# A written instruction order for the first sequence of a thresholded-attention and ELU-FFN kernel

## The chip, the cores and the metric

The kernel runs on one core of one Trainium2 chip. A core has five engines, each with a queue of its own: PE (TensorE, matrix products and transposes, into PSUM), DVE (VectorE), ACT (ScalarE), POOL (GpSimd) and SP (SyncE, which here issues the DMAs). They meet through semaphores. The metric is the device time of one execution in microseconds; lower is better.

## The reference

Two blocks follow each other. The attention block has 8 batch elements ("sequences") of 8 heads, 576 rows, head size 64. Of each row of scores only those within tau of the row's maximum are kept:

```
scores = scale * np.matmul(q, k.transpose(0, 1, 3, 2))
thresh = np.max(scores, axis=-1, keepdims=True) - tau
scores = np.where(scores >= thresh, scores, -1000000000.0)
attn = np.exp(scores - np.max(scores, axis=-1, keepdims=True))
attn = attn / (np.sum(attn, axis=-1, keepdims=True) + 1e-09)
return np.matmul(attn, v).astype(np.float32)
```

The result, 4608 tokens by 512, goes through `h = x @ w_in` (512 by 2048), an ELU, and `@ w_out` (2048 by 512). The two weight matrices arrive as 64-bit floats and are turned into 32-bit ones on the core.

## The kernel before

**Steps.** Two heads make a pair; a sequence has 4 pairs, all sequences 32. The 576 rows of a pair are worked in five steps, i = 0 to 4. Steps 0 to 3 take 128 rows of both heads; step 4 takes the last 64 rows of both heads as one tile of 128 rows (`heads_of(4)` is `[0]`). A sequence is thus 20 steps and 36 tiles of a head; `per_seq` is 20.

**One head of a step.** `scores` (L238, PE) writes 128 by 576 scores to PSUM. The row maximum `mx` (L248, DVE) gives `nb`, the negative scaled maximum (L249, POOL), and the threshold `th` (L250, POOL). The exponential `e` is on ACT (L253), with `nb` as its bias. The mask (L265, DVE) keeps `e` where the score reaches `th`, writes `w` and sums it into `sm`. DVE adds 1e-9 and takes the reciprocal `rs` (L267, L268), and POOL multiplies `w` by it (L274).

**From w to the output.** `turn_parts` turns `w` in three parts: PE transposes (L277) into a PSUM tile `rt`, and ACT copies it to `wTa` (steps 0 and 1) or `wTb` (steps 2 to 4) (L293). `values` multiplies the turned tiles with v (L384, L388) into a PSUM tile `pv`, once a pair for steps 0 and 1 (part 0) and once for steps 2 to 4 (part 1). ACT copies that to `xt`, for part 1 to `xs` as well (L395, L400). `behind(pr, i)` does this for a step that completes a part and nothing for the others.

**Loads.** `load` brings q, k and v of a pair by DMAs on SP: four for q (`qm`), four for k (`km`), four for v. DVE transposes q and k (`prep_q` L195, `prep_k` L200), and POOL makes small copies (`copy_q` L207, `copy_k` L212).

**Weights.** Each matrix is cut into 16 pieces. `load_w` brings one; its conversion has the parts `convert_rest` (ACT, L129), `convert_top` (DVE, L136 and L137), `convert_add` (POOL, L143), `convert_abs` (ACT, L148) and `convert_end` (DVE, L155). `progress` counts the pieces loaded and converted. In the first sequence, calls of `convert_w` take six pieces, one each at head tiles 12, 16, 20, 24, 28 and 32.

**Buffers.** In the first sequence PSUM holds three tiles of scores for one head each (pool `ps_s0`, six of eight banks) and two tiles shared by `rt` and `pv` (pool `ps_t`).

**Three stages and their order.** The first sequence (20 steps) runs by head tiles in a loop that calls `begin` (scores and exponential) of tile n+1 before `finish` (mask and normalization) of tile n. This loop isn't in a manual schedule: a scheduler puts its instructions in order on each engine. The second stage (15 steps, with the rest of the weights and the first FFN products) and the third are inside `tc.manual_schedule()`: there each engine has its instructions in the order of the code. The functions `max_of`, `bound_of`, `exp_of`, `mask_of` and `reciprocal_of` are defined for the third stage (L1076 to L1104); there `nb` is made by ACT (L1086).

Of the kernel before, what the change touches and what calls it, by code (L numbers as in the profile page):

```python
# [10 lines left out]
FP32 = mybir.dt.float32  # L11
# [3 lines left out]
ALU = mybir.AluOpType  # L15
# [4 lines left out]
def kernel(  # L20
# [55 lines left out]


    tau_sb = const.tile([P, 1], FP32, name="tau_sb")
    nc.sync.dma_start(tau_sb, tau.to_broadcast([P, 1]))
    pos = const.tile([P, 1], FP32, name="pos")  # L80
    nc.vector.tensor_scalar(pos, tau_sb, 0.0, None, ALU.is_ge)
    keep = const.tile([P, 1], FP32, name="keep")
    nc.vector.tensor_scalar(keep, pos, SCALE, None, ALU.mult)
    nkeep = const.tile([P, 1], FP32, name="nkeep")
    nc.vector.tensor_scalar(nkeep, pos, -SCALE, None, ALU.mult)
    far = const.tile([P, 1], FP32, name="far")
    nc.vector.tensor_scalar(far, pos, -FAR, FAR, ALU.mult, ALU.add)
    ntau = const.tile([P, 1], FP32, name="ntau")
    nc.vector.tensor_tensor(ntau, tau_sb, far, ALU.max)
    nc.vector.tensor_scalar(ntau, ntau, -1.0 / SCALE, None, ALU.mult)  # L90

    w_in_sb = const.tile([P, KJ, DF], FP32, name="w_in_sb")
    w_out_sb = const.tile([P, NFT, DM], FP32, name="w_out_sb")
# [17 lines left out]
    def load_w(ahead=2):  # L111
        i = progress[0]
        if i >= len(pieces) or i >= progress[1] + ahead:
            return
        progress[0] += 1
        src, dst, j, n = pieces[i]
        rows = src[j * P : (j + 1) * P]
        if src.dtype == FP32:
            nc.sync.dma_start(dst, rows[:, n : n + WN])
            return  # L120
        st = staged[i] = wstage.tile([P, WN, 2], U32, name="wst", bufs=4)
        nc.sync.dma_start(st.rearrange("p n w -> p (n w)"), rows.bitcast(U32)[:, 2 * n : 2 * (n + WN)])
# [6 lines left out]
            nc.scalar.mul(lo.bitcast(I32), lo, 2.0**-29)  # L129

    def convert_top(i):

        if i in staged:
            hi = staged[i][:, :, 1]
            top = tops[i] = wstage.tile([P, WN], U32, name="wtop", bufs=2)
            nc.vector.tensor_scalar(top, hi, 3, 0x3FFFFFFF, ALU.logical_shift_left, ALU.bitwise_and)  # L136
            nc.vector.scalar_tensor_tensor(top, hi, 0xC0000000, top, ALU.bitwise_and, ALU.bitwise_or)  # L137

    def convert_add(i):
# [14 lines left out]
            mag, top = staged.pop(i)[:, :, 1].bitcast(FP32), tops.pop(i).bitcast(FP32)  # L154
            nc.vector.scalar_tensor_tensor(pieces[i][1], mag, 1.125 * 2.0**-15, top, ALU.is_ge, ALU.mult)  # L155

    def convert_w():
        i = progress[1]
        if i >= progress[0]:
            return  # L160
        for f in (convert_top, convert_rest, convert_add, convert_abs, convert_end):
            f(i)
        load_w()


    raws, pairs = {}, {}


    def load(pr, parts=("qm", "km", "v"), shared=False):
        b, j = divmod(pr, NPAIR)  # L170
        tiles = raws.setdefault(pr, {})
        for name, src in (("qm", q), ("km", k)):
            if name not in parts:
                continue
            m = tiles[name] = raw.tile([P, S // T, T], FP32, name="qm" if shared else name)
            for i in range(2):
                for d in range(2):
                    r = (2 * i + d) * T
                    nc.sync.dma_start(
                        m[r : r + T],  # L180
                        src[b, 2 * j + i].rearrange("(j t) d -> t j d", t=T)[:, :, d * T : (d + 1) * T],
                    )
        if "v" not in parts:
            return
        vm = tiles["vm"] = raw.tile([P, 2, NC, D], FP32, name="vm", bufs=2)
        vd = tiles["vd"] = vds[pr % NVD]
        for i in range(2):
            vh = v[b, 2 * j + i]
            nc.sync.dma_start(vm[:, i], vh[:MAIN].rearrange("(c p) d -> p c d", p=P))
            r = slice(i * TAIL, (i + 1) * TAIL)  # L190
            nc.sync.dma_start(vd[r, r], vh[MAIN:])
# [22 lines left out]
    def prep(pr):  # L214
        for f in (prep_q, copy_q, prep_k, copy_k):
            f(pr)
# [5 lines left out]
    def scores(pr, i, hs):  # L222
        qT, kT, qd = pairs[pr]
        if hs[0] == 0:
            open_steps[pr, i] = {
                **{x: small.tile([P, 2], FP32, name=x) for x in ("mx", "nb", "th", "sm", "rs")},
            }
        st = open_steps[pr, i]
        if "f" in psum and not apart:
            both = psum["s"].tile([P, 2, 2, 512], FP32, name="sc")  # L230
            scs = {h: both[:, h] for h in hs}
        else:
            scs = {h: psum["s"].tile([P, 2, 512], FP32, name="sc") for h in hs}
        for a in range(2):
            for h in hs:
                k0 = a * HALF + (0 if h else TAIL)
                r, qs = (slice(h * D, (h + 1) * D), qT[:, i * P : (i + 1) * P]) if i < NC else (slice(0, P), qd)
                nc.tensor.matmul(scs[h][:, a, :HALF], qs[r], kT[r, k0 : k0 + HALF], start=True, stop=True)  # L238
        if len(hs) == 2 and not apart:
            st["both"] = both  # L240
        for h in hs:
            st[h] = scs[h]
# [27 lines left out]
    def normalize(pr, i, hs):  # L270
        st = open_steps[pr, i]
        for h in hs:
            wv = st["w"][:, h * S : (h + 1) * S]
            nc.gpsimd.tensor_scalar(wv, wv, st["rs"][:, h : h + 1], 1.0, ALU.mult, ALU.mult)  # L274

    def transpose(dst, src):
        nc.tensor.matmul(dst, src, ident, is_transpose=True, skip_group_check=True)  # L277

# [7 lines left out]


    def turn_parts(pr, i):
        w = open_steps.pop((pr, i))["w"]
        wT, g0 = turned_tile(pr, i)  # L290

        def to(gs, cs, src, r=slice(0, P)):
# [213 lines left out]
    def heads_of(i):  # L506
        return [0, 1] if i < NC else [0]
# [28 lines left out]
            for post in posts[engines]:  # L536
                post()

    def begin(*step):
        scores(*step)  # L540
        exponentials(*step)

    def finish(*step):
        masks(*step)
        normalize(*step)

    def ahead(pr, i):
        if i == 2 and pr + 1 < NP:
            prep(pr + 1)
        if i == 3 and pr + 2 < NP:  # L550
            load(pr + 2, ("qm", "km"))
        if i == 3 and pr + 1 < NP and pr:
            load(pr + 1, ("v",))

    load(0)
    prep(0)
    load(1)

    heads = [(pr, i, [h]) for pr, i in steps[:per_seq] for h in heads_of(i)]
    turned = deque()  # L560
    begin(*heads[0])
    for n, (pr, i, hs) in enumerate(heads):
        if n + 1 < len(heads):
            begin(*heads[n + 1])
        if n == 2:
            load_w()
            load_w()
        if n >= 12 and n % 4 == 0:
            convert_w()
        finish(pr, i, hs)  # L570
        if len(turned) > 1:
            behind(*turned.popleft())
        if n and hs == [0]:
            turn(*heads[n - 1][:2])
            turned.append(heads[n - 1][:2])
        if hs == [1]:
            ahead(pr, i + 1)
    first.close()
    for name, bufs in (("s", 1), ("f", 2)):
        psum[name] = banks.enter_context(tc.tile_pool(name=f"ps_{name}", bufs=bufs, space=PSUM))  # L580

    while len(turned) > 1:
        behind(*turned.popleft())

# [159 lines left out]
    with tc.manual_schedule():  # L746
# [326 lines left out]
                    at(end + lag, f)  # L1073
                n -= 1

        def max_of(pr, i, h):  # L1076
            st = open_steps[pr, i]
            nc.vector.tensor_reduce(st["mx"][:, h : h + 1], st[h][:, :, :HALF], axis=AX.XY, op=ALU.max)  # L1078

        def bound_of(pr, i, h):  # L1080
            st = open_steps[pr, i]
            nc.gpsimd.tensor_scalar(st["th"][:, h : h + 1], st["mx"][:, h : h + 1], 1.0, ntau, ALU.mult, ALU.add)  # L1082

        def exp_of(pr, i, h):
            st = open_steps[pr, i]
            nc.scalar.mul(st["nb"][:, h : h + 1], st["mx"][:, h : h + 1], nkeep)  # L1086
            e = att.tile([P, 2, HALF], FP32, name="e")
            nc.scalar.activation(e, st[h][:, :, :HALF], AF.Exp, bias=st["nb"][:, h : h + 1], scale=keep)  # L1088
            st[h] = st[h], e

        def mask_of(pr, i, h):
            st = open_steps[pr, i]
            if h == 0:
                st["w"] = wpool[0].tile([P, 2 * S], FP32, name="w")
            sc, e = st.pop(h)
            wv = st["w"][:, h * S : (h + 1) * S].rearrange("p (a n) -> p a n", a=2)
            nc.vector.scalar_tensor_tensor(wv, sc[:, :, :HALF], st["th"][:, h : h + 1], e, ALU.is_ge, ALU.mult,  # L1097
                                           accum_out=st["sm"][:, h : h + 1])

        def reciprocal_of(pr, i, hs):  # L1100
            st = open_steps[pr, i]
            cs = slice(hs[0], hs[-1] + 1)
            nc.vector.tensor_scalar(st["sm"][:, cs], st["sm"][:, cs], 1e-9, None, ALU.add)
            nc.vector.reciprocal(st["rs"][:, cs], st["sm"][:, cs])  # L1104

        begun = [0.0]

        def softmax(pr, i):
# [143 lines left out]
```

## Time and profile before

| what | us |
|---|---|
| median of 3 runs (lowest, highest) | 1387.35 (1385.84, 1392.01) |
| the profiled execution's own time | 1385.93 |
| its span in the profile | 1384.1 |

| engine | busy in the span, us | share |
|---|---|---|
| PE, matmuls | 1334.5 | 96% |
| DVE | 1066.5 | 77% |
| POOL | 827.5 | 60% |
| ACT | 632.4 | 46% |

All other numbers come from this profiled execution. Times are counted from the start of its span. A line of the timeline has a start, a duration, the engine, the line of the code, the operation, what it writes from what it reads with shapes, how many instructions were merged, and, in brackets, how long the engine stood idle before it and what released it. A line of the windows view has, for one stretch, the busy time and the number of instructions of PE, PE's weight loads, DVE, ACT and POOL, then the granted clock of PE, the share of the DMA engines and GB/s. Ends of matmuls are modelled, so a busy PE is not a PE at its peak. Float32 matmuls are recorded in two instructions each; transposes in one.

### The profile page before, as it was taken

How to read it: one execution, taken by the hardware profiler on the slowest of the kernel's cores; microseconds unless marked ns; L12 is line 12 of the kernel's file. 1: busy time of each engine (PE TensorE's matmuls, PEld its weight loads, DVE VectorE, ACT ScalarE, POOL GpSimd, SP SyncE). 2: the span in 40 equal slices, each digit the busy share in tenths (PEclk: the TensorE clock that was granted, in tenths of full speed). 3: DMA queues.
4: the chain of work that ended last, by engine and by line, in shares of the span. 5: the costliest groups of instructions: out<-in, count | busy, mean ns of one | idle time of the engine just before them, and what ended most of it. 6: DMA issues, size and time to landing. Idle time of an engine off the chain costs nothing.

```text
span 1384.1 us, 21954 instructions
## 1 busy us (share of the span) xinstructions
PE 1334.5 (96%) x6566; PEld 988.6 (71%) x6566; DVE 1066.5 (77%) x2362; ACT 632.4 (46%) x1387; POOL 827.5 (60%) x1331
## 2 busy tenths in 40 slices
PE   6897989999999999999999999999999999999998
PEld 4554745747777777777777777777777777888886
DVE  6877885988888887888788978888888874545533
ACT  4666654325454445445453636263635452422421
POOL 5667773878657564756475747675666656414422
PEclk9999999999999999999999999999999999999999
DMA  5245451688897979898888988897889785411211
GB/s 114 58 91 148 132 148 44 187 244 254 226 261 221 280 214 255 209 266 240 230 231 256 251 222 236 236 258 212 239 230 275 217 241 146 133 58 64 92 57 31
DMA packets 316342, 259.82 MB, mean 188 GB/s; under 512 B 208320, under 2 KB 272320, under 8 KB 316224
## 3 DMA queue, kind: packets, MB, share of 16 engines
q1 hardware_dynamic: 316224, 258.42, 67.4%
q8 instruction: 53, 0.87, 0.3%
q14 instruction: 65, 0.53, 0.1%
HBM read 167.84 MB, written 90.51 MB: 187 GB/s over the span
## 4 chain that ended last, share of the span: by engine, by line
PE 76%; DVE 9%; ACT 5%; POOL 4%; issue 3%; DMA 1%; SPq 1%; DVEq 0%; POOLq 0%; ACTq 0%
PE f L999 28%; PE f L846 21%; PE sc L238 11%; PE pv L388 9%; PE pv L384 2%; PE f L435 2%; PE f L475 2%; ACT e L1088 2%; DVE w L265 2%; ACT e L253 1%; DVE mx L1078 1%; PE rt L277 1%; POOL wtop L143 1%; DVE mx L248 1%; DVE wtop L137 1%
## 5 line engine op out<-in xcount | busy, mean ns | idle before, releaser
L274 POOL TENSOR_SCALAR w<-w,rs 128x576 f32<-128x576 f32 x288 | 246.2, 860 | 108.4 <-DVE rs L1104 75.1
L1078 DVE TENSOR_REDUCE mx<-sc 128x1 f32<-128x576 f32 x207 | 148.0, 751 | 82.6 <-PE sc L238 82.6
L238 PE MATMUL sc<-kT,qT 64*128 64x288 f32 x1024 | 182.6, 440 | 22.1 <-DVE w L265 11.9
L348 DVE STREAM_TRANSPOSE x<-w 128x512 f32<-128x512 f32 (+1 forms) x350 | 182.5, 567 | 8.2 <-POOL w L274 8.2
L1086 ACT ACTIVATE nb<-mx,nkeep 128x1 f32<-128x1 f32 x207 | 61.4, 297 | 253.4 <-DVE mx L1078 253.4
L1088 ACT ACTIVATE e<-sc,nb,keep 128x576 f32<-128x576 f32 x207 | 172.1, 831 | 6.9
L1097 DVE SCALAR_TENSOR_TENSOR w<-sc,th,e 128x576 f32<-128x576 f32 x207 | 163.0, 810 | 8.6 <-ACT e L1088 0.4
L238 PEld LDWEIGHTS sc<-kT,qT 64*128 64x128 f32 x1024 | 100.7, 191 | 87.2 <-issue 51.8
L846 PE MATMUL f<-xt,sw 128*128 128x256 f32 x512 | 129.0, 389 | 1.0 <-DVE ot L1017 0.5
L846 PE MATMUL f<-xt,w_in_sb 128*128 128x256 f32 x512 | 125.1, 383 | 1.7 <-ACT w L860 1.5
L1082 POOL TENSOR_SCALAR th<-mx,ntau 128x1 f32<-128x1 f32 x207 | 54.3, 263 | 111.6 <-DVE mx L1078 111.4
L846 PEld LDWEIGHTS f<-xt,sw 128*128 128x128 f32 x512 | 93.2, 190 | 29.8 <-issue 13.5
L846 PE MATMUL f<-x,w_in_sb 128*128 128x256 f32 x448 | 109.0, 382 | 5.5 <-ACT g L913 5.5
L253 ACT ACTIVATE e<-sc,nb,keep 128x576 f32<-128x576 f32 x81 | 65.1, 830 | 104.2 <-POOL nb L249 103.2
L846 PEld LDWEIGHTS f<-xt,w_in_sb 128*128 128x128 f32 x512 | 95.7, 190 | 22.1 <-ACT xs L400 4.6
L999 PE MATMUL f<-w_out_sb,s 128*128 128x256 f32 x448 | 109.4, 387 | 0.0
L999 PE MATMUL f<-t,s 128*128 128x256 f32 x448 | 106.7, 381 | 0.6 <-POOL s L939 0.6
L999 PE MATMUL f<-w_out_sb,g 128*128 128x256 f32 x448 | 107.2, 382 | 0.0
L846 PEld LDWEIGHTS f<-x,w_in_sb 128*128 128x128 f32 x448 | 84.1, 190 | 21.2 <-ACT g L913 10.2
L999 PEld LDWEIGHTS f<-w_out_sb,s 128*128 128x128 f32 x448 | 82.3, 190 | 23.0 <-issue 13.2
L999 PEld LDWEIGHTS f<-w_out_sb,g 128*128 128x128 f32 x448 | 84.0, 190 | 15.8 <-ACT ge L879 3.5
L999 PEld LDWEIGHTS f<-t,s 128*128 128x128 f32 x448 | 84.0, 190 | 14.3 <-POOL s L939 3.4
(162 smaller groups left out, 2543.6 us busy)
## 6 DMA issues: line engine op xcount, KB each, us to landing
there<-x SPq DMA_DIRECT2D x500, 144.0 KB, 4.2
wTb<-there SPq DMA_DIRECT2D x75, 576.0 KB, 4.6
wTa<-there SPq DMA_DIRECT2D x50, 576.0 KB, 4.3
sw<-win_sums SPq DMA_DIRECT2D x62, 384.0 KB, 4.7
t<-wout_sums SPq DMA_DIRECT2D x45, 512.0 KB, 5.4
qm<-in_q_dram SPq DMA_DIRECT2D x128, 72.0 KB, 4.2
vm<-in_v_dram SPq DMA_DIRECT2D x64, 128.0 KB, 4.2
wst<-in_moe_w_in_dram SPq DMA_DIRECT2D x16, 512.0 KB, 4.5
```

What stands on the lines that cost most here:

```text
L238: nc.tensor.matmul(scs[h][:, a, :HALF], qs[r], kT[r, k0 : k0 + HALF], start=True, stop=True)
L253: nc.scalar.activation(e, st[h][:, :, :HALF], AF.Exp, bias=st["nb"][:, h : h + 1], scale=keep)
L274: nc.gpsimd.tensor_scalar(wv, wv, st["rs"][:, h : h + 1], 1.0, ALU.mult, ALU.mult)
L348: nc.vector.transpose(x[:, :, c0 : c0 + nc_], src.rearrange("p (c g n) -> p g c n", c=nc_, n=T))
L388: nc.tensor.matmul(pv[h * D : (h + 1) * D, g0 * T : g1 * T], vm[:, h, c], wT[:, g0:g1, h * (NC + 1) + c], start=False, stop=(c == NC - 1), ...
L846: nc.tensor.matmul(loc["banks"][place], left[:, j], right[:, j], start=(begins and j == 0), stop=(j == 1), skip_group_check=True)
L999: nc.tensor.matmul(place(m), lhs, rhs, start=(begins and v == 0), stop=(v == RU - 1), skip_group_check=True)
L1078: nc.vector.tensor_reduce(st["mx"][:, h : h + 1], st[h][:, :, :HALF], axis=AX.XY, op=ALU.max)
L1082: nc.gpsimd.tensor_scalar(st["th"][:, h : h + 1], st["mx"][:, h : h + 1], 1.0, ntau, ALU.mult, ALU.add)
L1086: nc.scalar.mul(st["nb"][:, h : h + 1], st["mx"][:, h : h + 1], nkeep)
L1088: nc.scalar.activation(e, st[h][:, :, :HALF], AF.Exp, bias=st["nb"][:, h : h + 1], scale=keep)
L1097: nc.vector.scalar_tensor_tensor(wv, sc[:, :, :HALF], st["th"][:, h : h + 1], e, ALU.is_ge, ALU.mult, accum_out=st["sm"][:, h : h + 1])
```

## The change

It rewrites the first stage; the second and third are left as they are.

- The first stage is put into `tc.manual_schedule()` and goes by steps of two heads instead of by head tiles: one call of `scores` for both heads, then maximum, bound, exponential and mask of each head at written places, and one reciprocal for both.
- ACT makes `nb` of head 0 (`nc.scalar.mul`), POOL that of head 1.
- The turning of step n-1 stands in step n: its first part ahead of head 1, its others behind the scores of step n+1. `behind(n-2)` stands after the reciprocal. The five parts of a weight's conversion are spread over steps; the loads stand at steps i = 3 and 4.
- At the start q is issued first on SP, then tau, and k of the first pair on ACT's queue. The instructions that read tau come after the first transposes of q and k. PE makes 28 transposes of the identity into a tile that nobody reads.
- The functions of the third stage are moved up, and `exp_of` gets a parameter `on_pool`.

```diff
-    nc.sync.dma_start(tau_sb, tau.to_broadcast([P, 1]))
...
-    load(0)
-    prep(0)
-    load(1)
...
-    begin(*heads[0])
-    for n, (pr, i, hs) in enumerate(heads):
-        if n + 1 < len(heads):
-            begin(*heads[n + 1])
-        if n == 2:
-            load_w()
-            load_w()
-        if n >= 12 and n % 4 == 0:
-            convert_w()
-        finish(pr, i, hs)
-        if len(turned) > 1:
-            behind(*turned.popleft())
-        if n and hs == [0]:
-            turn(*heads[n - 1][:2])
-            turned.append(heads[n - 1][:2])
-        if hs == [1]:
-            ahead(pr, i + 1)
+    with tc.manual_schedule():
+        load(0, ("qm",))
+        nc.sync.dma_start(tau_sb, tau.to_broadcast([P, 1]))
+        load(0, ("km",), queue=nc.scalar)
+        load(0, ("v",))
+        load(1)
+
+        idle = psum["t"].tile([P, NC, P], FP32, name="rt", tag="rt")
+        for _ in range(28):
+            transpose(idle[:, 0], ident)
+        prep_q(0)
+        prep_k(0)
+        read_tau()
+        copy_k(0)
+        copy_q(0)
+        scores(0, 0, [0, 1])
+        for n in range(per_seq):
+            pr, i = steps[n]
+            hs = heads_of(i)
+            x = progress[1]
+            if n:
+                normalize(*steps[n - 1], [0])
+                turned = turn_parts(*steps[n - 1])
+            max_of(pr, i, 0)
+            exp_of(pr, i, 0)
+            bound_of(pr, i, 0)
+            if n:
+                copies = turned[0]()
+            if len(hs) == 2:
+                max_of(pr, i, 1)
+                st = open_steps[pr, i]
+                nc.gpsimd.tensor_scalar(st["nb"][:, 1:], st["mx"][:, 1:], nkeep, 1.0, ALU.mult, ALU.mult)
+            if n and len(heads_of(steps[n - 1][1])) == 2:
+                normalize(*steps[n - 1], [1])
+            if len(hs) == 2:
+                exp_of(pr, i, 1, True)
+                bound_of(pr, i, 1)
+            if n:
+                copies()
+
+            if i == NB - 1 and n + 1 < per_seq:
+                convert_top(x)
+                convert_add(x)
+            elif i == 0 and n:
+                convert_end(x)
+                load_w()
+            elif i == 1 and pr:
+                convert_sign(x)
+                convert_add(x)
+            elif i in (2, 3):
+                (prep_q if i == 2 else prep_k)(pr + 1)
+                (copy_q if i == 2 else copy_k)(pr + 1)
+            mask_of(pr, i, 0)
+            if n + 1 < per_seq:
+                scores(*steps[n + 1], heads_of(steps[n + 1][1]))
+            if n:
+                for part in turned[1:]:
+                    part()()
+            if len(hs) == 2:
+                mask_of(pr, i, 1)
+            reciprocal_of(pr, i, hs)
+            if n > 1 and steps[n - 2][1] in (1, NB - 1):
+                behind(*steps[n - 2])
+            if i == 0 and n:
+                convert_shift(x + 1)
+            elif i == 2 and pr:
+                convert_end(x)
+                load_w()
+            if (i == NB - 1 and n + 1 < per_seq) or (i == 1 and pr):
+                convert_abs(x)
+            if i == 3 and n + 2 < per_seq:
+                convert_rest(x)
+            elif i == NB - 1 and n + 1 < per_seq:
+                convert_rest(x + 1)
+            if i in (3, 4):
+                load(pr + 2, ("qm",) if i == 3 else ("km",))
+            if i == 3 and pr:
+                load(pr + 1, ("v",))
+            if n == 0:
+                load_w()
+                load_w()
+        for h in heads_of(steps[per_seq - 1][1]):
+            normalize(*steps[per_seq - 1], [h])
...
+    def exp_of(pr, i, h, on_pool=False):
+        st = open_steps[pr, i]
+        if not on_pool:
+            nc.scalar.mul(st["nb"][:, h : h + 1], st["mx"][:, h : h + 1], nkeep)
+        e = att.tile([P, 2, HALF], FP32, name="e")
+        nc.scalar.activation(e, st[h][:, :, :HALF], AF.Exp, bias=st["nb"][:, h : h + 1], scale=keep)
+        st[h] = st[h], e
```

`convert_shift` and `convert_sign` are the two instructions of `convert_top`, now to be called one by one; `load` takes the issuing queue as a parameter.

## The prediction

> **What bounds the kernel now.** I read the page first: TensorE is recorded busy for 96% of the span, but the change touches only the first of three stages, so the whole-span share says little. The chain of waits and the timeline put that stage between the first scores (8.21 us) and the first joint maximum of the next stage (106.82 us, "mx 128x2"); everything behind 106.82 is the same program. The windows of the stage, about one pair of heads each, with the columns PE, PEld, DVE, ACT, POOL, granted clock, DMA share, GB/s:
>
> ```profile
> 13.00:34.00 21.00, 19.11 (x89) 12.49 (x90) 17.48 (x52) 14.02 (x25) 14.25 (x31) 1.00 0.49 121
> 34.00:57.00 23.00, 21.27 (x114) 11.87 (x112) 18.59 (x52) 15.24 (x33) 14.68 (x31) 1.00 0.33 71
> 57.00:84.00 27.00, 25.03 (x114) 14.26 (x115) 19.23 (x53) 17.03 (x36) 15.41 (x33) 0.87 0.31 68
> 84.00:107.00 23.00, 21.09 (x117) 12.68 (x116) 17.88 (x53) 15.78 (x34) 15.78 (x31) 1.00 0.44 96
> ```
>
> PE is full at 91 to 93%, DVE at 71 to 83%, ACT at 63 to 69%; a pair takes 21 to 27 us, 23.5 on average. The waits between 8 and 107 us (total, times, longest):
>
> ```profile
> ACT e L253 <- POOL nb L249: 28.6, 19, 9.8
> DVE mx L248 <- PE sc L238: 13.3, 13, 2.5
> ACT xt L395 <- PE pv L388: 5.2, 3, 2.7
> ```
>
> DVE waits for scores, which stand behind other PE work; ACT is mostly early. The third line matters for the new order: ACT can stand still before the copy of a values product. The prices come from these lines of the timeline (start, duration):
>
> ```profile
> 22.41 1.23 PE L238 MATMUL sc<-kT,qT 64*128 64x288 f32 x4 [0.40 <-DVE w L265]
> 120.70 1.24 PE L238 MATMUL sc<-kT,qT 64*128 64x288 f32 x8 [0.17 <-DVE w L265]
> 82.00 0.66 PE L277 MATMUL rt<-ident,w 128*128 128x128 f32 x4
> 82.70 0.58 ACT L293 COPY wTb<-rt 128x512 f32<-128x512 f32 x1 [0.19 <-PE rt L277]
> 50.82 0.70 PE L384 MATMUL pv<-wTa,vd 128*128 128x256 f32 x2
> 51.45 1.95 PE L388 MATMUL pv<-wTa,vm 128*64 128x256 f32 x16
> 53.44 0.37 ACT L395 COPY xt<-pv 128x256 f32<-128x256 f32 x1 [1.14 <-PE pv L388]
> 507.10 0.29 ACT L1086 ACTIVATE nb<-mx,nkeep 128x1 f32<-128x1 f32 x1 [3.31 <-DVE mx L1078]
> 507.43 0.83 ACT L1088 ACTIVATE e<-sc,nb,keep 128x576 f32<-128x576 f32 x1
> 17.23 1.97 PE L277 MATMUL rt<-ident,w 128*128 128x128 f32 x8
> ```
>
> One head's scores take 1.23 us, both heads together 1.24: half the scores time on PE goes away. Four transposes and their copy follow each other within 0.04 us. A values product takes 2.6 us (50.82 to 53.40; part 1, with 320 columns, 3.2), and its copy starts 0.04 us behind it.
>
> **What the Trainium skill says.** "TensorE: Matmul & The Clock Gate", in the table under its title, has ScalarE, VectorE and GpSimdE as strict FIFO queues and PE reordering weight loads alone; the second stage here, also written by hand, agrees: its ACT instructions run in the order of the code. Its Part 3 ("The mechanism") lets tiles in different row groups run at the same time, as the two score lines show. Its Part 1 ("What's actually happening") halves the clock when PE has been idle and gives it back after some 3.4 us of work; the trace agrees in part: the recorded clock was 0.50 from 66 to 70 us, and eight transposes at 17.23 took 0.246 us each against 0.15 later, while the record still said 1.00. "DMA: Bandwidth & Descriptors", "Issuing engines are not separate DMA queues", says that a second issuing engine saves only issue time.
>
> **The start.** Before, SP issues tau, four q and four k DMAs at about 0.54 us each; the last k issue ends at 5.35, k lands at 7.38, its transpose ends at 8.17, scores start at 8.21. Now q leads on SP and k is issued beside it on ACT, so the last issue ends near 2.8; with the 2.05 us from there to landing both land near 5.0. Two DVE transposes (0.78 each) give kT at 6.6, the POOL copy of kT (0.23) 6.85. But the 28 idle transposes start with ident at 1.5 and stand ahead of the scores in PE's queue: cold 0.246 each, warm 0.15; with the clock coming at about 6.5 they end near 7.7 (6.9 if warm early; 8.4 if cold throughout). Scores 7.7 to 8.95, maximum to 9.7, ACT's nb and exponential to 10.9, first mask 11.0 to 11.8. The first mask ended at 13.94 before: 2.1 us gained. Reading tau (six DVE instructions, 0.85 us) lies under the scores. Issuing k costs ACT nothing, as it waits until 9.7.
>
> **A step.** Set t=0 at the end of head 0's mask of step n. Scores use three PSUM tiles, two a step, so those of n+1 need this mask. PE: scores 0.06 to 1.30, transposes of n-1, second half, to 1.96, the last to 2.2. DVE: second mask, sums, reciprocal to 1.22, maximum of n+1 from 1.34 to 2.08. ACT: the copies of those transposes, 2.0 to 2.64; only then nb, because it is behind them in ACT's queue. nb 0.32, exponential to 3.79, mask 3.89 to 4.71. A plain step takes 4.71 us; DVE is idle for over a microsecond of it.
>
> **Steps with values.** The values product of n-2 is written behind the transposes, and its copy ahead of the next step's nb. It needs the PSUM buffer of the second transposes, free at 2.6. Part 1 (step i=1 of a later pair): PE 2.64 to 5.85, copies of xt and xs to 6.6, convert_abs 0.63, nb 7.25, exponential to 8.4, mask to 9.3. What waits behind ACT's copy is nb, then both exponentials, then DVE's masks, then the scores after that: everything. Part 0 falls in step i=3, where the next step has one head and its scores find a free tile, so PE gets to the product earlier: product to 8.2 counted from the end of step i=2's mask, copy, convert_rest 0.63, nb 9.2, mask to 11.27; less the 4.71 of the plain step before it, 6.56. Step i=4: scores again early, but copies, abs and rest (0.65 each) on ACT hold nb: 3.56. Step i=0: the copies are short, DVE's convert_shift adds 0.45: 4.5. Step i=2: 4.75, with convert_end on DVE. Five steps: 6.56 + 3.56 + 4.5 + 9.3 + 4.75 = 28.7 us a pair, against 23.5 before.
>
> **Sum.** First mask 11.8; three steps of the first pair 4.17 + 4.71 + 4.71 = 13.6; three rounds of 28.7 = 86.0; last transition (part 0, no convert_rest) 5.9: last mask ends at 117.3. The next stage's scores follow at once (0.06 + 1.24), DVE's convert_top fits beside, and the maximum starts at 118.8: 12.0 us later than 106.82. Before, it took 3.4 us from the last mask to that maximum; that gain of 1.9 is in the sum. Weights: six pieces converted and eight loaded on both sides, so the next stage begins in the same state. POOL gives one nb in two to ACT (0.26) and is nowhere late. On SP the same loads stand in nearly the same order: q of the first pair is no longer behind tau, v and the next pair no longer behind k, and the first weight DMAs (14.56 before) still come after them; all are needed a step or more later. I cost these moves at nothing: SP idles through most of the stage (DMA share 0.31 to 0.49), and without that slack the weights would be late first, at step 3, some 14 us on.
>
> **The clock.** The stage before has one half-speed stretch, 64 to 71 us. After, PE idles 2.9 us in each part-1 step (from 6.45 to 9.36), and a pause of 1.9 us at 198 us was followed by half speed. Half speed in the step behind costs 1.24 + 0.6 = 1.85 us on the path; three of these 5.6, and up to 9 with a slow product too. Against it, the old stretch, worth up to 4, may be gone. From -4 to +9, I take +1. Forecast: +13. The profiled execution took 1385.93 us (span 1384.1 and 1.8 around it), so 1399; the median of the three runs, 1387.35, lies 1.4 above that execution: 1400.
>
> **Rivals.** First, faster: the values product is hidden, because its copy does not hold ACT (if ACT's order or PE's differs from the code, or the copies find time ahead of the maximum). Without it the steps are 3.7 + 3.7 + 4.5 + 5.3 + 4.7 = 21.9 a pair; last mask at 11.8 + 13.6 + 65.7 + 3.1 = 94.2, maximum at 95.7, 11 us earlier: 1376. For it: PE's halved scores, DVE's 71 to 83%. Against: the order in the code. The case decides for the slower side once the products and conversions on ACT add over 11.1/3 = 3.7 us a pair. Second, about even: half of each product is covered, say because the second transposes go ahead of the scores: 1388. Third, slower still: half clock recurs in most steps, +20: 1407. Fourth, the stage's gain is lost later because the weights' conversion or DMAs set the next stage: then even a faster start gives 1387; the equal counts of pieces speak against it.
>
> **Chances.** Forecast, 1394 to 1404: 0.45. Half clock, up to 1412: 0.15. About even or lost later: 0.2. Faster: 0.2. A measurement of this kernel tells a change from none at about 0.5%, 7 us. So slower 0.6, same 0.2, faster 0.2. The likeliest case alone spans 1394 to 1404; to leave out no more than two in ten the range reaches from 1378, within the faster case, to 1412.
>
> **What would show it.** The first score near 7.7 (7 to 8.4), eight records in 1.24; ACT's xt copy waiting over 2 us for PE, seven times, and nb right behind it; gaps of 4 to 5 us on DVE ahead of the mask in steps i=2; pairs of 28 to 29 us; the first "mx 128x2" near 119. I am wrong if pairs take 22 us, if nb stands ahead of the xt copy on ACT, or if the next stage takes back the delay: it lasts 112 us (107 to 219) and should keep that.

## The result and the profile after

| | before | after |
|---|---|---|
| median of 4 runs, us | 1389.53 | 1422.62 |
| lowest to highest, us | 1385.84 to 1392.01 | 1420.54 to 1425.68 |
| ratio to before, 95% interval | | 1.0242 (1.0207 to 1.0277) |
| profiled execution, us | 1385.93 | 1420.54 |
| first joint maximum ("mx 128x2"), us | 106.82 | 139.78 |

The changed kernel is slower by 33 us. The first joint maximum of the second stage comes 33.0 us later, so nearly all of it arises in the first stage and stays to the end (the two profiled executions lie 34.6 us apart). Forecast were 118.8 us for that point and 1400 for the time; 21 us of delay in the first stage are unaccounted for by the forecast.

The page of the kernel after: the span, the engines' busy time, and the granted TensorE clock in 40 slices of 35.5 us.

```profile
span 1418.7 us, 21934 instructions
...
PE 1353.2 (95%) x6594; PEld 998.2 (70%) x6594; DVE 1068.8 (75%) x2330; ACT 636.1 (45%) x1407; POOL 822.8 (58%) x1311
...
PEclk7877999999999999999999999999999999999999
```

Before, the clock's row was 9 throughout. Now the first four slices, which are the first stage, read 7 and 8. PE's busy time grew by 18.7 us although the only new work is the 28 idle transposes (4.65 us), and a step's scores take 1.24 us once where they took it twice: a matmul at half clock counts as busy for longer. "PE 95%" therefore doesn't say that PE did more.

The windows of three equal rounds of five steps, from the mask of head 0 of step 3 to that of step 8, then 13, then 18 (PE, PEld, DVE, ACT, POOL, granted clock, DMA share, GB/s):

```profile
28.33:60.79 32.46, 24.87 (x115) 14.01 (x115) 19.80 (x46) 17.69 (x40) 13.95 (x25) 0.82 0.25 55
60.79:95.43 34.64, 27.36 (x115) 15.44 (x115) 19.67 (x46) 17.47 (x40) 15.58 (x30) 0.75 0.30 63
95.43:129.59 34.16, 26.39 (x115) 14.96 (x115) 20.98 (x47) 18.58 (x42) 16.28 (x27) 0.75 0.27 57
```

A pair takes 32.5 to 34.6 us; the forecast had 28.7, before it was 23.5. Each shows the clock at 0.75 to 0.82, that is half speed for 36 to 50% of the round.

The waits of the first stage (engine, line, who released it: total, times, longest), between 5 and 150 us:

```profile
DVE w L295 <- ACT e L286: 32.2, 6, 8.1
ACT xt L423 <- PE pv L416: 25.8, 7, 5.7
...
ACT wTa L321 <- PE rt L305: 18.0, 7, 3.1
...
PE sc L235 <- DVE w L295: 14.2, 10, 2.6
```

ACT's wait for the values product, 5.2 us in 3 times before, is now 25.8 in 7. DVE's masks wait 32.2 us for the exponential, 0.9 us once before. The last line, 14.2 us, was 2.8 us in 4 times before: PE itself stands still for scores that wait for a mask.

One step with part 1 of a values product, in the timeline of the kernel after (start, duration, what; in brackets the idle time before it):

```profile
44.13 0.82 DVE L295 SCALAR_TENSOR_TENSOR w<-sc,th,e 128x576 f32<-128x576 f32 x1
...
46.60 1.40 DVE L275 TENSOR_REDUCE mx<-sc 128x1 f32<-128x576 f32 x2
...
48.15 0.75 ACT L321 COPY wTa<-rt 128x512 f32<-128x512 f32 x2 [2.56 <-PE rt L305]
...
48.79 1.65 PE L412 MATMUL pv<-wTb,vd 128*128 128x384 f32 x2 [0.46 <-ACT wTa L321]
...
50.37 3.22 PE L416 MATMUL pv<-wTb,vm 128*64 128x320 f32 x16
...
53.63 0.37 ACT L423 COPY xt<-pv 128x256 f32<-128x256 f32 x1 [4.73 <-PE pv L416]
...
54.34 0.67 ACT L153 ACTIVATE wst<-wst 128x512 f32<-128x512 f32 x1
...
54.92 0.28 ACT L284 ACTIVATE nb<-mx,nkeep 128x1 f32<-128x1 f32 x1
55.23 1.55 ACT L286 ACTIVATE e<-sc,nb,keep 128x576 f32<-128x576 f32 x2
...
56.15 0.82 DVE L295 SCALAR_TENSOR_TENSOR w<-sc,th,e 128x576 f32<-128x576 f32 x1 [7.47 <-ACT e L286]
...
57.03 1.23 PE L235 MATMUL sc<-kT,qT 64*128 64x288 f32 x6 [2.19 <-DVE w L295]
```

The two maxima of the next step run from 46.60 to 48.00; `nb`, which needs nothing but the first of them, starts at 54.92, because it stands behind the copy `xt` in ACT's queue, which waits 4.73 us for the product. From mask to mask 12.0 us go by. The forecast had this chain, with 9.3 us. The product is slower than it assumed: 1.65 + 3.22 us where full speed gave 3.2 in all. And the line of 57.03 shows that PE then pauses 2.19 us, waiting for the mask.

### The profile page after: what moved, and what is told of

Read it like the earlier page. It is cut to its first block, busy times and chain, and to the rows that moved or that the text cites. A ratio compares the mean times of both kernels' runs of the same rounds, so it can differ in the third digit from the quotient of the medians.

```text
span 1418.7 us, 21934 instructions
## 1 busy us (share of the span) xinstructions
PE 1353.2 (95%) x6594; PEld 998.2 (70%) x6594; DVE 1068.8 (75%) x2330; ACT 636.1 (45%) x1407; POOL 822.8 (58%) x1311
## 4 chain that ended last, share of the span: by engine, by line
PE 74%; DVE 9%; ACT 7%; DMA 4%; POOL 3%; issue 3%; SPq 1%; DVEq 0%; ACTq 0%; POOLq 0%
PE f L1071 27%; PE f L918 18%; PE sc L235 11%; PE pv L416 9%; PE pv L412 3%; ACT e L286 2%; PE f L463 2%; PE f L503 2%; DMA there<-x 2%; DVE mx L275 2%; DVE w L295 2%; PE rt L305 1%; DVE w L262 1%; ACT e L250 1%; ACT nb L284 1%
## 5 line engine op out<-in xcount | busy, mean ns | idle before, releaser
L275 DVE TENSOR_REDUCE mx<-sc 128x1 f32<-128x576 f32 x243 | 174.2, 751 | 85.0 <-PE sc L235 84.8
L295 DVE SCALAR_TENSOR_TENSOR w<-sc,th,e 128x576 f32<-128x576 f32 x243 | 191.6, 811 | 57.5 <-ACT e L286 32.6
L235 PE MATMUL sc<-kT,qT 64*128 64x288 f32 x1024 | 178.7, 447 | 27.3 <-DVE w L295 14.2
L286 ACT ACTIVATE e<-sc,nb,keep 128x576 f32<-128x576 f32 x243 | 200.7, 831 | 8.2 <-POOL nb L600 0.2
L284 ACT ACTIVATE nb<-mx,nkeep 128x1 f32<-128x1 f32 x227 | 67.3, 296 | 262.4 <-DVE mx L275 262.4
L235 PEld LDWEIGHTS sc<-kT,qT 64*128 64x128 f32 x1024 | 97.3, 193 | 94.0 <-issue 53.5
L279 POOL TENSOR_SCALAR th<-mx,ntau 128x1 f32<-128x1 f32 x243 | 64.8, 267 | 116.2 <-DVE mx L275 115.6
L937 POOL TENSOR_TENSOR u<-u,w 128x256 f32<-128x256 f32 x64 | 49.1, 768 | 69.3 <-ACT u L932 65.8
```

The source lines that it names most:

```text
L937: nc.gpsimd.tensor_tensor(loc[name], x(), loc[other], op)
```

## The experiments

The theory after the result had two parts. One: ACT's copy of the product holds `nb`, as forecast. Two: the pauses that the new order leaves on PE keep its clock at half speed in most of the stage. The rivals: that there is one cause alone, and the other goes when it goes; that PE's product, not ACT's copy, is what is in the way; that the start did it. The first eight kernels were run once each, beside one execution of before on the same chip (1390.40 us for the first four, 1387.87 for the others); those times have no interval and are read with the traces. Where transposes are added to fill pauses, they go into a PSUM tile or a column of one that nobody reads, like the 28 of the change.

**The copies late.** The product stays where it is, and ACT's copies of it go behind the exponentials of the next step.

```diff
             if n > 1 and steps[n - 2][1] in (1, NB - 1):
-                behind(*steps[n - 2])
+                held.append(values(steps[n - 2][0], 0 if steps[n - 2][1] == 1 else 1))
...
+            while held:
+                held.pop()()
             if n:
                 copies()
```

> The values products stay where the change puts them on PE; only ACT's copies of them move, behind the exponentials of the next step. Queue theory (the copy, waiting on ACT ahead of nb, holds the whole next step): the step behind a part-1 product shrinks by about 2.8 us and the pair's part-0 and i=4 steps together by about 1.9, 4.7 a pair, so the joint maximum of the next stage comes near 126 instead of 139.8 and the time near 1408. Clock theory alone (only PE's half speed makes the stage long, ACT would wait anyway): 139 to 141, time unchanged at about 1421.

1407.23 us, joint maximum at 126.78: 13.0 earlier than in the kernel after, as the queue theory had it. The part-1 step of the same place in the timeline of this kernel:

```profile
49.51 0.69 ACT L153 ACTIVATE wst<-wst 128x512 f32<-128x512 f32 x1
...
50.08 0.30 ACT L284 ACTIVATE nb<-mx,nkeep 128x1 f32<-128x1 f32 x1
50.41 1.55 ACT L286 ACTIVATE e<-sc,nb,keep 128x576 f32<-128x576 f32 x2
...
51.09 2.40 PE L416 MATMUL pv<-wTb,vm 128*64 128x320 f32 x8
51.33 0.82 DVE L295 SCALAR_TENSOR_TENSOR w<-sc,th,e 128x576 f32<-128x576 f32 x1 [2.06 <-ACT e L286]
```

`nb` and both exponentials now run while the product is still on PE, and the step (mask at 44.63 to mask at 51.33) takes 6.7 us instead of 12.0. The clock stays low (0.74 on average from 8 to 127 us, as in the kernel after from 8 to 140). So ACT's order costs 13 us at that clock, and the half clock is not its by-product.

**The pauses filled.** The order stays that of the change; 44 idle transposes at the start, and filling ones behind `behind(n-2)` in every step.

```diff
+            for _ in range(12 if n == 0 else 11 if n == 1 else (14, 18, 3, 0, 18)[i]):
+                transpose(last_room[0][:, 3], ident)
```

> The change with transposes of the identity put into PE's idle stretches at the end of each step (12, 11, 14, 18, 3, 0 or 18 by step) and 44 instead of 28 at the start; nothing else differs. Clock theory (half speed after pauses is what the prediction's walk lacked): the recorded clock stays at 1.0 in the stage, plain steps take 4.7 us, the step behind a part-1 product 9.3, and the joint maximum comes near 119, time near 1400. Queue theory alone (the steps are that long at any clock): 138 or later, as the added work lies on PE.

1406.59 us, joint maximum at 127.04: 12.7 earlier than after, and 8 later than expected. Its windows of two rounds, step 3 to 8 and 8 to 13:

```profile
26.75:55.03 28.28, 24.96 (x169) 16.99 (x168) 19.81 (x46) 17.83 (x40) 14.27 (x27) 1.00 0.31 65
55.03:83.28 28.25, 24.93 (x169) 16.98 (x168) 19.80 (x45) 17.83 (x40) 14.76 (x28) 1.00 0.34 71
```

At clock 1.00 a pair takes 28.3 us (the third round, with some half clock, 31.2). That is the forecast's 28.7 with the same order on ACT, so its walk through the steps stands, and what the kernel after has above it, 32.5 to 34.6, goes with the clock. The missing 8 us: three other steps still ran partly at half clock (6.3 us from 15.80 on, 11.0 from 97.95, 7.6 from 114.49; 4.3 us more in all than the same steps at full clock), and 18 filling transposes of the last step stood ahead of the second stage's scores, as its timeline shows:

```profile
123.65 2.19 PE L305 MATMUL rt<-ident 128*128 128x128 f32 x18
125.77 1.23 PE L235 MATMUL sc<-kT,qT 64*128 64x288 f32 x6
...
127.04 1.36 DVE L245 TENSOR_REDUCE mx<-sc 128x2 f32<-128x1152 f32 x1 [3.74 <-PE sc L235]
```

Those 2.2 us are a cost of the experiment. With both added to the 12.7, half clock is worth about 19 us in the kernel after, an estimate from these lines.

**The product first.** The product stands at the head of the next step on PE, its copies behind that step's exponentials.

```diff
+            if n > 1 and steps[n - 2][1] in (1, NB - 1):
+                held.append(values(steps[n - 2][0], 0 if steps[n - 2][1] == 1 else 1))
             if n:
                 normalize(*steps[n - 1], [0])
...
+            while held:
+                held.pop()()
             if n:
                 copies()
...
-            if n > 1 and steps[n - 2][1] in (1, NB - 1):
-                behind(*steps[n - 2])
```

> The values products go to the head of their step, ahead of the transposes, into a stretch where PE waits for the mask; their copies go behind that step's exponentials on ACT. Queue theory: no step waits for a product any more, part-1 steps fall from 12 to 6 or 7 us, the joint maximum near 120 even with half-speed stretches, and near 100 if the better filled PE keeps its clock. Clock theory alone: the clock drops as before and the maximum stays above 135.

1414.90 us, joint maximum at 132.83; neither number was met. The main wait is another now, and one stretch of the timeline says why:

```profile
DVE mx L275 <- PE sc L235: 25.8, 12, 4.2
```

```profile
43.30 1.65 PE L412 MATMUL pv<-wTb,vd 128*128 128x384 f32 x2 [0.74 <-ACT wTb L321]
...
44.88 3.77 PE L416 MATMUL pv<-wTb,vm 128*64 128x320 f32 x16
...
49.16 1.24 PE L235 MATMUL sc<-kT,qT 64*128 64x288 f32 x8
...
50.44 1.42 DVE L275 TENSOR_REDUCE mx<-sc 128x1 f32<-128x576 f32 x2 [4.07 <-PE sc L235]
```

A product at half clock, 5.3 us, stands ahead of the next scores. The kernel is 7 us better than the change, in which `nb` stood behind the waiting copy, and 6 us worse than with the product left in its place and only the copies late. Where the product stands on PE thus matters as well; in the change itself what held the chain was the copy, as the late copies show.

**The start alone.** The kernel before with only the change's first lines: q, tau and k issued in the new way, 28 idle transposes, and tau read later.

```diff
-    load(0)
-    prep(0)
-    load(1)
+    with tc.manual_schedule():
+        load(0, ("qm",))
+        nc.sync.dma_start(tau_sb, tau.to_broadcast([P, 1]))
+        load(0, ("km",), queue=nc.scalar)
+        load(0, ("v",))
+        load(1)
...
+        for _ in range(28):
+            transpose(idle[:, 0], ident)
+        prep_q(0)
+        prep_k(0)
+        read_tau()
```

> The kernel before with the new start alone (q first, k on ACT's queue, 28 idle transposes, tau read later), the rest of its stage in the scheduler's order. If the start is worth what the prediction said, the first mask ends near 11.8 and the time falls by 2 us; as the changed kernel's trace has the first scores at 8.24 against 8.21, I expect the scores there again, a gain of 0 to 2 us from a warm clock in the first steps, time 1384 to 1388.

1386.04 us, first mask at 11.56 (13.13 before), joint maximum at 104.64, 2.2 earlier than before. So the start didn't cost the 33 us; the loss is in the loop. What the start gains is smaller than this one trace shows (see the timed runs).

**Both.** The late copies and the filling together, with 14 transposes behind the first scores and none in the last step.

```diff
+        for _ in range(14):
+            transpose(idle[:, 0], ident)
...
+            for _ in range(12 if n == 0 else 11 if n == 1 else 0 if n == per_seq - 1 else (14, 0, 3, 0, 10)[i]):
+                transpose(last_room[0][:, 3], ident)
```

> The change with both edits: ACT's copies of the products behind the next exponentials, and PE's idle stretches filled with transposes of the identity (44 at the start, 14 behind the first scores, then 12, 11, 14, 0, 3, 0 or 10 by step, none in the last). If ACT's order and the clock are two causes that stand beside each other, a pair takes 28.3 - 4.7 = 23.6 us and the joint maximum comes near 105 to 108; if one of them already held what the other frees, it stays near 124.

1394.02 us, joint maximum at 113.02: 26.8 earlier than in the kernel after. That is close to the sum 13.0 + 12.7, though this filling is not that of the filled kernel and leaves out the 2.2 us of the last step. The two effects add up, so neither contains the other. The time fell short of the expected 105 to 108: a pair takes 25.3 us at clock 1.00, where 23.6 were expected, and 27.0 and 27.3 in the two later rounds, which have 3.4 us of half clock each. At the joint maximum 6.2 us over the kernel before are left; the two rounds with half clock, 1.7 and 2.0 us over the first, are part of that.

**Transposes early.** The kernel of the last run; eight of the nine transposes of a turning, and the normalization of both heads that they need, go ahead of the next scores, and fewer filling ones are left.

```diff
-                normalize(*steps[n - 1], [0])
+                normalize(*steps[n - 1], heads_of(steps[n - 1][1]))
...
             if n:
                 copies()
+                turned[1]()()
...
-                for part in turned[1:]:
+                for part in turned[2:]:
...
-            for _ in range(12 if n == 0 else 11 if n == 1 else 0 if n == per_seq - 1 else (14, 0, 3, 0, 10)[i]):
+            for _ in range(5 if n == 0 else 4 if n == 1 else 0 if n == per_seq - 1 else (4, 0, 2, 0, 6)[i]):
```

> The kernel of the run before, with the second transposes and both normalizations of a step ahead of the next scores instead of behind them, so that ACT's copies no longer stand between the maximum and nb. By the walk a plain step falls from 4.7 to 4.2 us and a pair to 21 to 22: joint maximum 96 to 100, time about 8 us below the kernel before. If the steps stay at 4.7, ACT's copies were not what held them.

1386.80 us, joint maximum at 104.92, clock 1.00 throughout the stage. A plain step takes 4.24 us, a pair 23.8 to 25.1: no better than the 23.5 of the old loop. The expected 96 to 100 was not reached. The 8.1 us against the kernel before it are the order, the smaller filling and the last half clock together; no run separates them.

**The idle transposes.** Taken from the kernel before with the new start, and from the change.

```diff
-        for _ in range(28):
-            transpose(idle[:, 0], ident)
```

> The kernel before with the new start (q first, k on ACT's queue, tau read later) but without the 28 idle transposes. If the 2.2 us that the start gained come from a warm PE, the first scores take over 2 us again and the first mask ends near 13.9; if they come from earlier keys, it ends at 12.4 as with the transposes. The first scores start near 8.2 in both.

> The change without its 28 idle transposes. If they only help in the first step, the first mask comes 1 to 2 us later and everything behind by as much: joint maximum 141 to 142. If PE's cold start costs more than one step in this order, several us more; if nothing, 139 to 140.

Before with the new start: 1384.31 us, first mask 12.97, joint maximum 103.36. The change without them: 1421.03, first mask 12.50, joint maximum 140.52. They bring the first mask 0.9 to 1.4 us forward. At the joint maximum the change lost 0.7 us without them while the other kernel gained 1.3; both are less than two traces of one kernel can differ by (below).

**Timed runs.** The last four kernels were run more often, in turn with before (median 1388.71 us of 51 runs). The first is the order of "transposes early" without any filling; the others repeat kernels from above.

> Order of the sixth run (all transposes of a step's turning and both normalizations ahead of the next scores, product's copies late) without any filling transposes. If the half clock is kept by the pauses alone and the filling was what removed it, the half clock comes back in some of the first stage: joint maximum at 110 to 116, 1392 to 1398 us. If the shorter steps leave too few pauses for it, and the filling only stood in the way, the joint maximum comes below 104.9, at 100 to 104, and the time at 1382 to 1386.

> The kernel before with the new start alone, timed. If the 2.2 us gained at the joint maximum stay to the end, the ratio to before is 0.997 to 0.999; if the later stages take them back, 1.000.

> The same without the idle transposes, timed. If the idle transposes are worth the 1 us at the first mask that the single looks showed, this one is 1 us slower than the run with them; if its lead of 1.3 us at the joint maximum was more than the accident of one half-clock stretch, it is 1 to 2 us faster.

> The sixth run's kernel, timed: the changed order with late copies, early transposes and few filling transposes. From its single look, ratio 0.998 to 1.001: equal to before.

| kernel | median, us | runs | ratio to before, 95% | joint maximum, us |
|---|---|---|---|---|
| order, late copies, early transposes, no filling | 1388.76 | 14 | 1.0002 (0.9992 to 1.0013) | 106.69 |
| the same with filling | 1386.06 | 12 | 0.9980 (0.9971 to 0.9989) | 104.89 |
| before with the new start | 1386.20 | 22 | 0.9987 (0.9978 to 0.9996) | 106.26 |
| before with the new start, no idle transposes | 1384.23 | 15 | 0.9972 (0.9960 to 0.9984) | 106.26 |

Without filling the joint maximum fell between the two values expected, and the time is 2.7 us longer than with it: the half clock came back, for less. What PE does between 8 and 16 us shows how the filling works; first without it, then with it:

```profile
8.05 1.72 PE L235 MATMUL sc<-kT,qT 64*128 64x288 f32 x10 [1.65 <-DVE pos L82]
12.36 2.25 PE L235 MATMUL sc<-kT,qT 64*128 64x288 f32 x6 [2.60 <-DVE w L295]
14.54 1.75 PE L305 MATMUL rt<-ident,w 128*128 128x128 f32 x7
```

```profile
8.08 1.62 PE L235 MATMUL sc<-kT,qT 64*128 64x288 f32 x8
9.63 1.75 PE L305 MATMUL rt<-ident 128*128 128x128 f32 x14
11.30 0.75 PE L235 MATMUL sc<-kT,qT 64*128 64x288 f32 x2
12.39 1.21 PE L235 MATMUL sc<-kT,qT 64*128 64x288 f32 x6 [0.34 <-DVE w L295]
```

The same six score instructions take 2.25 us behind a pause of 2.60 and 1.21 us behind the filling. The best kernel is the old loop with the new start and no idle transposes: 4.5 us faster than before, 0.3%. Three of these kernels have two traces each, and these show what one trace is worth: "transposes early" with filling has the joint maximum at 104.92 and 104.89, but the new start at 104.64 and 106.26, and without idle transposes at 103.36 and 106.26. Differences of up to 3 us at the joint maximum are therefore not to be laid on a change; the 13.0, 12.7 and 26.8 lie far above that.

Why the new start is 2.0 us better without the idle transposes, though its first mask comes over a microsecond later, isn't settled. The two profiled executions took 1385.50 us with them and 1385.74 us without, so their traces don't show the difference of the medians. They do show that half-clock stretches differ between executions: with the idle transposes about 13 to 16 and 61 to 71 us, without them 86 to 93, and in the earlier trace without them none from 50 to 106. No run here controls these stretches.

## Why the prediction was right or wrong

**Direction and mechanism: right, but not the whole.** The copy of a values product stands ahead of `nb` on ACT. ACT waits for the product seven times, 2.5 to 5.7 us each, and moving the copies alone takes 13.0 us away. The Trainium skill's statement that ScalarE is a strict queue ("TensorE: Matmul & The Clock Gate", table under the title), on which this rested, holds in the timeline: `nb` at 54.92 right behind the conversion at 54.34. But either cause alone would have made the change slower (126.78 without the first, 127.04 with most of the second gone, against 106.82), and with the copies late and all but 6.8 us of the half clock gone the joint maximum still came at 113.02. The written order became as fast as the old loop only with the transposes ahead as well. The first rival's 21.9 us a pair was reached in no run of the written order.

**"A step" and "steps with values": right at full clock.** With filling, the steps of a pair took 6.67, 3.36, 4.37, 9.24 and 4.64 us; forecast were 6.56, 3.56, 4.5, 9.3 and 4.75.

**"The start": half right.** The first mask started 1.55 us earlier, against 2.1 forecast. The landing "near 5.0" for q and k was wrong. So was the reason for the first scores at 7.7, that the idle transposes would end there: they ended at 6.11, and the scores waited for q and k. The start of the kernel after in its timeline:

```profile
0.73 2.13 ACTq L176 DMA_DIRECT2D km<-in_k_dram  x4
...
0.73 2.02 SPq L176 DMA_DIRECT2D qm<-in_q_dram  x4
...
1.46 4.65 PE L305 MATMUL rt<-ident 128*128 128x128 f32 x28 [1.46 <-POOL ident masks.py:199]
...
6.75 0.78 DVE L192 STREAM_TRANSPOSE qT<-qm 128x576 f32<-128x576 f32 x1 [6.75 <-DMA qm<-in_q_dram]
...
8.24 1.26 PEld L235 LDWEIGHTS sc<-kT,qT 64*128 64x128 f32 x10 [2.37 <-DVE pos L82]
```

Issue ended at 2.75 and 2.86 as forecast, but q landed at 6.75, four microseconds later, where it had taken 2.2 before (issued until 3.22, landed 5.41). I had kept the old time to landing for twice as many transfers at once. The page of the Trainium skill that I cited ("DMA: Bandwidth & Descriptors", "Issuing engines are not separate DMA queues") has them all run on the same 16 DMA engines, and I used only its sentence on issue time. That the sharing made q late fits this, but no run has the two loads apart. First scores thus start at 8.24, as before (8.21). What is gained lies behind them: the maximum comes sooner since the scores of both heads end 1.7 us after their start; 0.9 us of the 1.55 were gone without the idle transposes.

**"The clock": the failed step.** It priced half speed from -4 to +9 and took +1: half speed in the step behind a part-1 product, three times. Measured against the forecast's own walk, the kernel after is late by 0.6 us at the end of the first mask (12.40 against 11.8), by 3.2 in the first three steps (16.75 against 13.59), by 15.2 in the three rounds (101.26 against 86.1) and by 2.1 in the last transition (8.02 against 5.9): 21.1 in all (the walk's 118.8 doesn't contain the +1). By the estimate from the filled kernel about 19 of them are clock. The price of a step was about right (6.2 us instead of 4.71 for a plain one, 1.5 where I had 1.85; the part-1 steps 12.0 to 12.4 instead of 9.3, which was my "slow product"). The count was wrong: 12 of the 19 steps took over half a microsecond longer than at full clock. I expected half speed only behind the product. Yet the walk itself left PE idle in every plain step, for about 1.9 of 4.71 us (2.2 us of scores and transposes, and 0.66 for the first transposes), so PE was to be busy for 61% of it; I used the walk for the path alone. In the kernel after the clock falls eight times between 10 and 130 us, and in the 3.41 us before these falls PE is recorded busy for 40 to 64%. Three of them, in the windows of these 3.41 us (same columns as above):

```profile
41.87:45.29 3.42, 1.91 (x10) 1.05 (x11) 3.11 (x7) 2.76 (x7) 2.69 (x6) 1.00 0.01 2
69.18:72.59 3.41, 1.38 (x8) 0.76 (x8) 3.07 (x8) 3.30 (x8) 1.89 (x4) 1.00 0.00 0
103.31:106.73 3.42, 1.53 (x7) 0.72 (x7) 2.80 (x8) 3.31 (x7) 1.89 (x4) 1.00 0.00 0
```

The rival "half clock recurs in most steps" named the right state and gave it 7 us more than the forecast, where it costs about 19.

**The moves "at nothing", POOL and the weights: right but for 0.6 us.** The 33.0 us at the joint maximum are the 33 of the whole, so the second stage neither lost nor took back anything much. Within the first stage one piece of the weights was late: ACT stood 1.73 us for its DMA until 127.15, `nb` came behind it at 128.34, and the step took 5.27 us where the same step of the first round took 4.64. In the filled kernel the same wait, 1.99 us, made it 5.54; that is 0.9 of the 8 us that this kernel lacked.

**The half clock that stays.** This is where the first steps went, in windows of 1 us of the kernel after (same columns):

```profile
9.00:10.00 1.00, 0.96 (x8) 0.50 (x5) 0.49 (x1) 0.00 (x0) 0.13 (x1) 1.00 0.76 126
10.00:11.00 1.00, 0.00 (x0) 0.00 (x0) 0.93 (x2) 0.66 (x2) 0.27 (x1) 1.00 0.73 118
11.00:12.00 1.00, 0.00 (x0) 0.00 (x0) 0.42 (x1) 1.00 (x2) 0.51 (x2) 0.57 0.91 147
12.00:13.00 1.00, 0.45 (x2) 0.48 (x4) 1.00 (x3) 0.18 (x1) 0.00 (x0) 0.50 0.83 133
```

PE pauses from 9.96 to 12.55 for the first mask, and the clock falls at about 11.1, before it resumes. It is back only at about 31.6 us, ahead of the first values product, three steps later. In between a plain step takes 6.2 us, since its scores and transposes are slower and the masks wait for them. In the old loop PE was recorded busy for 91 to 93% of a pair; it had another head's scores to do in such gaps.

## What to carry to other kernels

When an order written by hand makes PE's work shorter, add up PE's pauses in every step as well as the path: in this kernel the clock fell where PE was recorded busy for 40 to 64% of 3.4 us, and the next steps then paid at half speed for the time that was saved. Single long pauses are not needed for that. An engine's copy of a long product belongs behind the short instruction that the next step waits for, if its queue is in order (13.0 us here). Time an independent part of a change alone: here the few lines at the start were a gain of 0.1% with the idle transposes and 0.3% without, which the loop had buried.

## What was not expected of the hardware

- Half clock came after shorter pauses than I had read from the Trainium skill. Its "TensorE: Matmul & The Clock Gate", Part 1, "What's actually happening", has the clock fall after an idle window of about 3.4 us. Here it fell 1.2 us into a pause of 2.59 us, and four of the eight falls (the three shown above and the one at 79.4 us) have no pause over 1.5 us in the 3.4 us before them. The page's later section "A second HAM failure mode: psum-queue depth-cycling", which lets frequent short pauses bring it about, agrees with this trace; I had not used it. No sharp bound comes out: from 35.03 to 38.44 PE is recorded busy for 56%, and the clock stayed.
- The half clock comes in whole units. Its eight stretches in the kernel after, from 11.1 to 134 us, are recorded as 20.5, 6.8, 3.4, 3.4, 6.8, 6.8, 13.7 and 6.8 us long, all multiples of 3.41 us. A short lack of work thus cost at least 3.4 us of half speed here.
- It stayed through more work than that page's 3.4 us of activity. From 14.74 to 20.46 us PE is recorded busy without a break, 5.7 us, at 0.50 throughout; ends of matmuls are modelled, so the record may hide gaps.
- At half clock the scores of both heads took 3.3 to 3.4 us for eight instructions, against 1.24: 2.7 times, not twice. Part of it can be a wait inside the group; the traces don't tell.
- A slow PE at the start isn't seen in the recorded clock. In the new start without idle transposes the first twelve score instructions took 4.20 us, with them 2.21, and the clock reads 1.00 in both. In the change without idle transposes it reads 1.00 from the start to 44 us, yet the scores of both heads took as long as at half clock until about 27 us:

```profile
16.70 3.42 PE L235 MATMUL sc<-kT,qT 64*128 64x288 f32 x8
...
22.95 3.32 PE L235 MATMUL sc<-kT,qT 64*128 64x288 f32 x8
...
33.99 1.24 PE L235 MATMUL sc<-kT,qT 64*128 64x288 f32 x8
```

  A reading of 1.00 ahead of a kernel's first recorded fall therefore doesn't show full speed. The first three steps took the same 4.39, 6.21 and 6.15 us with and without the idle transposes.
- Four q and four k DMAs issued side by side from two queues let q land 4.0 us after its last issue; one after the other on one queue it had been 2.2.
